# A two-layer transformer prompt on one core: PE transposes for the second unit's rows, held weight loads, new priorities

## The chip, the core and the metric

The program runs on one core of one Trainium2 chip. The time is device microseconds (us) of that core; the time of a kernel is the median over its runs. One further execution was recorded by the hardware profiler, and everything below that names an instant is an instant of that execution. Its engines are PE (TensorE matmul; its weight loads are shown apart as PEld), DVE (VectorE), ACT (ScalarE), POOL (GpSimd) and SP (SyncE, which here only issues transfers; ACT issues some as well).

## The reference

Two layers, each of them an attention block and a dense block on 2048 rows of 640 values:

```python
x = x + A(layernorm(x));  x = x + B(layernorm(x))      # twice, same weights

# A: 32 heads of 20, each row attends to itself and the 255 rows before it
qkv    = (x @ wqkv).reshape(B, S, 3, 32, 20)
scores = q @ k^T * 20 ** -0.5, masked to 0 <= i - j < 256
out    = (softmax(scores) @ v) @ wo

# B: squared ReLU
h   = relu(x @ w1 + b1) ** 2          # 640 -> 1536
out = h @ w2 + b2                     # 1536 -> 640
```

## The kernel before

**Units.** The work is cut into 16 units (`NU`): 2 layers times 8 groups of 256 rows (`T`). "The first unit" is unit 0. A unit goes through these stages. `layernorm` normalises its rows (two blocks of 128 rows). The rows are then transposed so that the 640 columns lie on the partitions, and split into a high and a low fp16 part (`yT`); each product below is three fp16 matmuls (`mm3`, L334). `stage_qk` computes q and k, which leave PSUM through one ACT and one DVE instruction (`high`, `low`, L534 and L537) into a staging tile, go to DRAM (`write`, L583 and L585) and come back in the layout of the heads (`spread`, L589). `stage_v` computes v. Attention runs in 8 "quads" of four heads: scores for the row maxima (`max_quad`, PE lines L703 and L735), the maxima sent into the q rows (`max_out` or `max_cross`, then `rows_out` L757), scores again and their exponentials (`exp_quad`: PE L840 and L886, ACT L825), masks on POOL or DVE, and the product with v (`pv_quad`, PE L931, then L943 and L946). The rows of the result go to DRAM (L951) and `load_o` brings them back (L984 the sums, L985 the rows) and divides by the sums in four slices (L1017, L1020, L1024, L1027: the job `od`). `stage_o` multiplies by `wo` and adds the residual (L1056); a second `layernorm`; a transposition into `y2` by `stage_y` or `y_cross`; `stage_f` is the dense block.

**Two ways to transpose.** `split_t` (L382) transposes on PE: five 128x128 transposes for a block of 128 rows, in tiles of three and two, into PSUM, and an ACT copy (L389) and a DVE subtraction (L390) take each tile out. `cross` (L443) writes the high part on ACT (L452) and the low part on DVE (L456) to a staging tile and transposes these with transfers issued by SP (L459). Before the change, unit 0 takes the first way (`ln_t(0)`), units 1 and 2 the second (`ln_early`).

**What sets the order.** All five engines run an order that is written out when the program is made. The program keeps a model of time: `post` adds a job with an engine, a cost, the jobs it depends on and a priority (`prio`; lower goes first); `pump` puts those jobs whose modelled start has come into the engine's stream. `dma` adds a transfer issued by SP, `bulk` a weight load issued by ACT, which is `idle`: it starts only when the modelled transfers are nearly done. The priorities are in the table `urgency` (L332), which is replaced once at unit 1 (L1381). The model decides only where an instruction stands in its engine's stream; what it waits for on the chip is its data and its tile.

**PSUM.** Results of the dense products and of `split_t` share two banks ("mm", `mm_tile` L240). PE can't begin a third until one of the two has been emptied.

**The dict `left`** (L540 to L555) holds, for a staging tile, the writes that must have left it before the next evictions overwrite it. Its test at L543 compares a pair with a tuple that holds a pair, which is never equal, so that in the model each piece of q (or k) of unit 0 waits for the write of the piece before it.

**Start and flow.** PE first runs `spin` matmuls without use. `load_wq` loads and converts the qkv weights (L285, L271, L272). `flow` (L1301) then runs the 8 quads of unit 0 (`todo`: maxima "m" three quads ahead, then "s" and "v") and, whenever the next step isn't ready in the model, takes a piece of the generator `rest` (`ahead_all`, L1350): q, k and v of units 0, 1 and 2 with the layernorms of units 1 and 2 between them. Under it, `load_wo`, `load_w1` and `load_w2` bring the other weights (ACT issues at L300, L309, L324). `load_w2` uses two places in the v tiles and three in the tile of unit 2's k rows; the latter is then filled with constants (`set_row`, L107) and with unit 2's k (L589). After `flow`, `load_o(0)` follows (L1368).

**From unit 1 on** (L1378), `together` runs the quads of unit u beside a chain of dense stages: for unit 1 `until(rest, ...)`, `stage_o(0)`, more of `rest`, `stage_y(0, ...)`, `stage_f(0)`; for units 2 to 14 `stage_qk` and `stage_v` of unit u+1 around `stage_o(u-1)` and `y_cross(u-1)`, then `stage_f(u-1)`. Unit 14 leaves `CARRY` ns of its dense work to unit 15; unit 15 spends it in portions: 10e3 (`MID`) before `stage_o(14)`, 4e3 after it, 2e3 between the two blocks of `stage_y(14)`, and what is left after the second block (L1392).

Of the kernel before, what the change touches and what calls it, by code (L numbers as in the profile page):

```python
# [16 lines left out]
P = 128  # L17
Q = P // 2
S = 2048
# [5 lines left out]
T = 256  # L25
# [6 lines left out]
NQ = H // 4  # L32
# [13 lines left out]
def kernel(ctx: ExitStack, tc: tile.TileContext, x, wqkv, wo, w1, b1, w2, b2, out):  # L46
# [70 lines left out]
    rate, apart, SWITCH = [335.0], [False], 110.0  # L117
    TAIL = {"A": 115.0, "D": 85.0, "G": 40.0, "S": 0.0}

    class Job:  # L120
        def __init__(self, eng, cost, fn, deps, nb, prio, size=0, idle=False, land=LAND):
            self.eng, self.cost, self.fn, self.deps, self.nb, self.prio = eng, cost, fn, deps, nb, prio
# [1 line left out]
            self.end, self.gates = None, []  # L124

        def ready(self):
            return all(d.end is not None for d in self.deps)

        def start(self):
            t = max([clk[self.eng], self.nb] + [d.end + LAT for d in self.deps])  # L130
            return max(t, moved[0] - 2200.0) if self.idle else t

        def put(self):
            t = self.start() + self.cost
# [194 lines left out]

    urgency = {"out": 0, "od": 1, "cross": 1, "mask": 0, "turn": 1, "exp": 1, "ln": 1, "y": 0.5, "clear": 0.5}  # L332

    def mm3(acc, lhs, rhs, nk, ns, then=None):  # L334

# [166 lines left out]
    def stage_qk(u, which=(0, 1)):  # L502
        js = pre.pop(u, ())
        yield Want(*js, bank=False)
        need(*js)
        yT = yTs[u]
        qds = {}

        order = [(j, c0) for j in which for c0 in range(0, KC, 2)]
        if u == 0:  # L510
            order.sort(key=lambda t: t[1])
        for j, c0 in order:
            if j not in qds:
                if j == 0:
                    qts[u] = sb.tile([P, NP, T], F16, name="qt", tag="qt", bufs=2)
                if j and u < 2:
                    qd, k = side(0), "side0"
                elif u == 2 and not j and opened0:
                    qd, k = side(1), "side1"
                elif j and u > 2:  # L520
                    qd = beside(u)[:, 1].rearrange("p (c a n) -> p c a n", a=2, n=T)
                    k = None
                else:
                    qd, k = sb.tile([P, KC, 2, T], F16, name="qd", tag="qd", bufs=1), "qd"
                qds[j] = qd, k
            qd, k = qds[j]
            dst = kts[u % 3] if j else qts[u]
            n = min(2, KC - c0)
            yield Want()
            acc, jobs = mm_tile([P, 2, T], "acc")  # L530
            s = QS / (YS * WS)

            def high(qd=qd, acc=acc, c0=c0, n=n):
                nc.scalar.activation(qd[:, c0:c0 + n, 0, :], acc[:, :n, :], AF.Copy, scale=s)  # L534

            def low(qd=qd, acc=acc, c0=c0, n=n):
                nc.vector.scalar_tensor_tensor(qd[:, c0:c0 + n, 1, :], acc[:, :n, :], s, qd[:, c0:c0 + n, 0, :],  # L537
                                               op0=ALU.mult, op1=ALU.subtract)

            def evict(wait, k=k, n=n, c0=c0, high=high, low=low, jobs=jobs, j=j, dst=dst, qd=qd):  # L540
                pr = urgency["out"]
                old = left.get(k, ())
                if k and (j, u) != old[:1]:  # L543
                    old = left[k] = ((j, u), [], old[1] if old else [])
                hi_ = post("A", 60 + 212 * n, high, *(old[2] if k else ()), wait=wait, prio=pr)
                lo_ = post("D", 70 + 267 * n, low, hi_, prio=pr)
                jobs.append(lo_)
                if u == 0:
                    wrote = leave(u, j, dst, qd, lo_, c0, n)
                elif c0 + n == KC:  # L550
                    wrote = leave(u, j, dst, qd, lo_, 0, KC)
                else:
                    return
                if k:
                    old[1].append(wrote)  # L555

            for c in range(n):
                lo = j * D + (c0 + c) * P
                need(wqj[lo // P])
                yield from mm3(acc[:, c, :], lambda a, k: wq_s[:, a, k, lo:lo + P],  # L560
                               lambda b, k: yT[:, b, k, :], KC, 109, evict if c == n - 1 else None)
# [11 lines left out]
    def leave(u, j, dst, qd, ready, c0, n):  # L573

        if c0 == 0:
            rows_of[u, j] = tc.dram_tile([D, 3, T], F16, name=f"qk{u}_{j}")
        dr = rows_of[u, j]
        drv = dr.rearrange("(c p) t n -> p c t n", p=P)

        p0, p1 = c0 * P // (2 * DH), (c0 + n) * P // (2 * DH)  # L580

        def write():
            nc.sync.dma_start(drv[:, c0:c0 + n, j:j + 2, :].rearrange("p c t n -> p c (t n)"),  # L583
                              qd[:, c0:c0 + n].rearrange("p c a n -> p c (a n)"))
            nc.sync.dma_start(drv[:, c0:c0 + n, 2 - 2 * j, :], qd[:, c0:c0 + n, 0, :])  # L585

        def spread():
            for e in range(2):
                nc.sync.dma_start(dst[64 * e:64 * e + 3 * DH, p0:p1, :],  # L589
                                  dr.rearrange("(p e d) t n -> e (d t) p n", e=2, d=DH)[e][:, p0:p1])  # L590

        wrote = dma(write, n * P * 3 * T * 2, ready, n=2, prio=0)

        def load(*deps):
            job = dma(spread, int((p1 - p0) * 2 * DH * 3 * T * 2 * (1.7 if u > 2 else 1.28)), wrote, *deps, n=2, prio=0)
            for p in range(p0, p1, 2):
                trips[u, j, p // 2] = job
            if u == 0 and j == 1 and p1 == NP:
                job.gates.append(gate)
            if u == 0 and j == 1 and p0 == 0:  # L600
                job.gates.append(gate0)

        if u == 2 and 2 not in rowset:
            held.append((j, load))
        else:
            load(*(rowset.get(u, ()) if j else ()))
        return wrote
# [361 lines left out]
    def load_o(u, late=False, free_=()):  # L969
# [15 lines left out]
            nc.sync.dma_start(val, ods[u][:DH].rearrange("(c d) h n -> (d h) c n", d=4))  # L985

        loaded = dma(load, P * (KC + 1) * T * 4, *wrote, *free_, n=2, prio=0)
        if u == NU - 1:
            both = sb.tile([P, 2, D], F32, name="x1", tag="qt", bufs=2)
            x1 = [both[:, i] for i in range(2)]  # L990
# [305 lines left out]
                if s.go() is None and not s.over:  # L1296
                    wait_any(s.want)

    QKC, VC, OC, FCST, LNC, CARRY, KEEP, MID = 16.4e3, 8.2e3, 8.2e3, 39.2e3, 1.2e3, 18e3, 24e3, 10e3

    def flow(todo, dense):  # L1301

# [2 lines left out]
        while todo:  # L1305
# [19 lines left out]
            elif kind == "s":  # L1325
                quad = exp_quad(n)
            else:
                pv_quad(n, quad)
            pump()

# [18 lines left out]

    def ahead_all():  # L1350
        yield from stage_qk(0)
        ln_early(1, place)
        yield from stage_v(0, range(2))
        ln_load(2)
        yield from stage_v(0, range(2, 4))
        ln_early(2)
# [14 lines left out]
    while not all(j.end is not None and j.end <= now[0] + LOOK for j in bbjobs):  # L1371
        c = next(rest)
        if not isinstance(c, Want):
            used[0] += c
            step(c)
    left_over = 3 * (QKC + VC) - used[0]
    rate[0] = 320.0
    for u in range(1, NU):  # L1378
        last = u == NU - 1
        if u == 1:  # L1380
            urgency.update({"out": 0, "od": 1.5, "cross": 1, "mask": 0, "turn": 0.7, "exp": 0.7, "ln": 0.5, "y": 1, "clear": 0.5})  # L1381
        quads, ahead = range(NQ * u, NQ * (u + 1)), range(NQ * u + LEAD, NQ * (u + 1) + LEAD)
        parts, cost, ahead_ln = [], OC + FCST, u + 2 if u + 2 < NU else None
        if 1 < u < NU - 1:
# [44 lines left out]
```

## Time and profile before

| | us |
|---|---|
| median of 3 runs | 1560.23 (1559.91 to 1561.74) |
| the profiled execution | 1561.46 |
| its span, first to last instruction | 1559.6 |
| so outside the span | 1.86 |

| engine | busy us | share |
|---|---|---|
| PE | 1533.5 | 98% |
| PEld | 1198.6 | 77% |
| DVE | 1043.3 | 67% |
| ACT | 669.7 | 43% |
| POOL | 451.8 | 29% |

A row of the timeline gives start, duration, engine, line, operation, output<-input and a count; the bracket at its end is the idle time of that engine before it and what ended it. A busy share says nothing about the clock: the windows view gives the granted TensorE clock (PEclk, 1.00 is full speed) of a stretch beside the busy time.

### The profile page before, as it was taken

How to read it: one execution, taken by the hardware profiler on the slowest of the kernel's cores; microseconds unless marked ns; L12 is line 12 of the kernel's file. 1: busy time of each engine (PE TensorE's matmuls, PEld its weight loads, DVE VectorE, ACT ScalarE, POOL GpSimd, SP SyncE). 2: the span in 40 equal slices, each digit the busy share in tenths (PEclk: the TensorE clock that was granted, in tenths of full speed). 3: DMA queues.
4: the chain of work that ended last, by engine and by line, in shares of the span. 5: the costliest groups of instructions: out<-in, count | busy, mean ns of one | idle time of the engine just before them, and what ended most of it. 6: DMA issues, size and time to landing. Idle time of an engine off the chain costs nothing. (4 is left out here: it accounts for less than half of the span.)

```text
span 1559.6 us, 58897 instructions
## 1 busy us (share of the span) xinstructions
PE 1533.5 (98%) x25822; PEld 1198.6 (77%) x25822; DVE 1043.3 (67%) x2244; ACT 669.7 (43%) x1365; POOL 451.8 (29%) x847
## 2 busy tenths in 40 slices
PE   8998999999999999999999999999999999999999
PEld 6666778787787877878777787877878777786777
DVE  8878775666757667675666757667675676667642
ACT  4565435334453443435343453444435335354422
POOL 1223314232141331413224141321413214142412
PEclk9999999999999999999999999999999999999999
DMA  9975354352534424344462434425243342542120
GB/s 271 209 201 127 80 121 92 106 114 54 123 88 114 105 74 126 69 126 89 99 130 63 119 91 119 100 70 132 67 126 89 94 117 65 122 90 59 30 68 18
DMA packets 248745, 162.16 MB, mean 104 GB/s; under 512 B 96552, under 2 KB 232232, under 8 KB 248488
## 3 DMA queue, kind: packets, MB, share of 16 engines
q1 hardware_dynamic: 242120, 148.89, 38.7%
q10 hardware_dynamic: 6368, 9.50, 2.1%
q8 instruction: 202, 3.31, 0.9%
q14 instruction: 55, 0.45, 0.1%
HBM read 84.68 MB, written 52.95 MB: 88 GB/s over the span
## 5 line engine op out<-in xcount | busy, mean ns | idle before, releaser
L825 ACT ACTIVATE pt<-bb 128x640 f32<-128x640 f32 (+2 forms) x512 | 311.9, 684 | 167.6 <-PE bb L840 148.9
L854 POOL TENSOR_SCALAR_AFFINE_SELECT pt<-pt 64x256 f32<-64x256 f32 x448 | 199.3, 445 | 582.1 <-ACT pt L825 560.0
L339 PE MATMUL acc<-y,w_s 128*128 128x256 f16 x2880 | 330.2, 274 | 1.2 <-DVE y L390 1.2
L339 PE MATMUL acc<-w_s,hh 128*128 128x320 f16 (+1 forms) x2340 | 326.7, 297 | 0.1
L339 PEld LDWEIGHTS <-w_s 128*128 128x128 f16 x2880 | 276.4, 98 | 40.9 <-issue 2.0
L339 PEld LDWEIGHTS <-hh 128*128 128x128 f16 x2340 | 222.1, 98 | 86.8 <-issue 0.4
L720 DVE TENSOR_REDUCE mx<-bb 128x4 f32<-128x1024 f32 x224 | 273.2, 1224 | 6.8
L339 PE MATMUL acc<-yT,wq_s 128*128 128x256 f16 x2250 | 259.1, 273 | 3.0 <-DVE qd L537 1.2
L339 PEld LDWEIGHTS <-wq_s 128*128 128x128 f16 x2400 | 229.6, 98 | 37.3 <-issue 4.3
L863 DVE COPY_PREDICATED_SCALAR pt<-drop,zero 128x256 f32 x224 | 99.9, 497 | 134.3 <-ACT pt L825 133.8
L1130 DVE TENSOR_TENSOR hh<-r,hh 128x256 f16<-128x256 f32 x192 | 98.3, 525 | 110.8 <-ACT hh L1127 105.7
L931 PE MATMUL pv<-pt,vt 64*32 64x192 f32 (+5 forms) x3840 | 166.7, 302 | 0.9 <-DVE y L390 0.6
L943 ACT COPY ot<-pv 128x256 f32<-128x256 f32 x128 | 47.6, 372 | 276.1 <-PE bb L931 247.2
L1124 POOL TENSOR_TENSOR r<-r 128x256 f32<-128x256 f32 x192 | 121.9, 655 | 127.9 <-ACT r L1120 125.3
L931 PE MATMUL bb<-pt,vt 64*32 64x128 f32 (+3 forms) x3584 | 153.5, 301 | 0.0
L717 DVE COPY_PREDICATED bb<-maskq,bb 128x256 f32<-128x256 uint16 x224 | 93.8, 423 | 85.7 <-PE bb L703 80.0
L931 PEld LDWEIGHTS pv<-pt,vt 64*32 64x32 f32 (+1 forms) x3840 | 125.5, 106 | 31.7 <-issue 3.7
L339 PE MATMUL acc<-wo_s,od 128*128 128x320 f16 x960 | 139.6, 299 | 2.2 <-ACT od L1024 2.0
L339 PE MATMUL acc<-wq_s,yT 128*128 128x320 f16 x900 | 132.1, 302 | 5.0 <-DVE qd L537 4.2
L1120 ACT ACTIVATE r<-acc,b1s 128x256 f32<-128x256 f32 x192 | 81.1, 476 | 98.6 <-PE acc L339 96.5
L339 PEld LDWEIGHTS <-od 128*128 128x128 f16 x960 | 90.9, 98 | 40.6 <-ACT od L1024 2.3
L339 PEld LDWEIGHTS <-yT 128*128 128x128 f16 x900 | 87.1, 98 | 40.0 <-issue 6.2
(103 smaller groups left out, 1476.3 us busy)
## 6 DMA issues: line engine op xcount, KB each, us to landing
qt<-qk SPq DMA_DIRECT2D x30, 480.0 KB
kt<-qk SPq DMA_DIRECT2D x30, 480.0 KB
o<-ot SPq DMA_DIRECT2D x256, 42.0 KB
qk<-qd SPq DMA_DIRECT2D x15, 640.0 KB
od<-o SPq DMA_DIRECT2D x14, 640.0 KB
qk<-yl SPq DMA_DIRECT2D x13, 640.0 KB
xt<-in_A_x_dram SPq DMA_DIRECT2D x16, 320.0 KB
x<-in_A_x_dram SPq DMA_DIRECT2D x16, 320.0 KB
```

The source lines that it names most:

```text
L339: nc.tensor.matmul(acc, lhs(a, c), rhs(b, c), start=(k == 0), stop=(k == 3 * nk - 1))
L717: nc.vector.copy_predicated(wins[:, :, 4 * Q:], later, wins[:, :, :Q])
L720: nc.vector.tensor_reduce(most, wins[:, :, Q:], axis=mybir.AxisListType.X, op=ALU.max)
L825: return lambda: nc.scalar.activation(room_of(box)[:, a:b], bank[:, a:b], AF.Exp, scale=SCALE / (QS * QS))
L854: nc.gpsimd.affine_select(out=m, in_=m, pattern=[[0, 4], [-1 if k else 1, Q]], base=0, fill=0.0, compare_op=ALU.is_gt if k else ALU.is_ge, ...
L863: nc.vector.copy_predicated(m, drop[:, k:k + 1, :].bitcast(mybir.dt.uint16).to_broadcast([P, 4, Q]), zero.unsqueeze(1).to_broadcast([P, 4, ...
L931: nc.tensor.matmul(pv[h][32 * jj:32 * (jj + 1), q0 * Q:(q0 + w) * Q], vf[r, c:c + 32], boxes[e]["pt"][r, a:b], start=(k == 0), stop=(k == ...
L943: nc.scalar.copy(ot[:, qd % 2], to)
L1120: nc.scalar.activation(box["r"], acc[:, f, :], AF.Relu, bias=b1s[:, f0 + f:f0 + f + 1], scale=1.0 / (YS * WS))
L1124: nc.gpsimd.tensor_tensor(box["r"], box["r"], box["r"], op=ALU.mult)
L1130: nc.vector.tensor_sub(hh[:, 1, f, :], box["r"], hh[:, 0, f, :])
```

## The change

The change has six parts.

1. The test at L543 now compares like with like: all pieces of one q (or k) share one entry, and wait only for the writes of the previous user of that staging tile.
2. In `ahead_all`, unit 1's rows are transposed by `ln_t(1, place)` on PE after the first half of `stage_v(0)`, in place of `ln_early(1, place)` (transfers) before it. Unit 2's still go by transfers. `left_over` grows by `LNC`.
3. A list `quiet` holds one empty job from the moment at which the last quad of unit 0 is about to be multiplied with v. `load_o(0)` ends it: the job's end is the modelled landing of the attention rows. Until then no `bulk` load is put into ACT's stream.
4. Writes of unit 2's q or k rows that are made while `quiet` has an entry wait for the same job.
5. Both tables of priorities change.
6. `CARRY` goes from 18e3 to 22e3.

```diff
+    quiet = []
...
         def ready(self):
-            return all(d.end is not None for d in self.deps)
+            return all(d.end is not None for d in self.deps) and not (self.idle and any(q.end is None for q in quiet))
...
-            return max(t, moved[0] - 2200.0) if self.idle else t
+            return max([t, moved[0] - 2200.0] + [q.end for q in quiet]) if self.idle else t
...
-    urgency = {"out": 0, "od": 1, "cross": 1, "mask": 0, "turn": 1, "exp": 1, "ln": 1, "y": 0.5, "clear": 0.5}
+    urgency = {"out": 0, "od": 0.5, "cross": 2, "mask": 0.5, "turn": 1, "exp": 1, "ln": 1, "y": 1, "clear": 0.5}
...
-                if k and (j, u) != old[:1]:
+                if k and (not old or old[0] != (j, u)):
                     old = left[k] = ((j, u), [], old[1] if old else [])
...
-        wrote = dma(write, n * P * 3 * T * 2, ready, n=2, prio=0)
+        wrote = dma(write, n * P * 3 * T * 2, ready, *(quiet if u == 2 else ()), n=2, prio=0)
...
         loaded = dma(load, P * (KC + 1) * T * 4, *wrote, *free_, n=2, prio=0)
+        if u == 0:
+            loaded.gates.append(quiet[0])
...
-    QKC, VC, OC, FCST, LNC, CARRY, KEEP, MID = 16.4e3, 8.2e3, 8.2e3, 39.2e3, 1.2e3, 18e3, 24e3, 10e3
+    QKC, VC, OC, FCST, LNC, CARRY, KEEP, MID = 16.4e3, 8.2e3, 8.2e3, 39.2e3, 1.2e3, 22e3, 24e3, 10e3
...
             else:
+                if n == NQ - 1:
+                    quiet.append(Job("S", 0.0, None, [], 0.0, 0))
                 pv_quad(n, quad)
...
         yield from stage_qk(0)
-        ln_early(1, place)
         yield from stage_v(0, range(2))
+        yield from ln_t(1, place)
         ln_load(2)
         yield from stage_v(0, range(2, 4))
         ln_early(2)
...
-    left_over = 3 * (QKC + VC) - used[0]
+    left_over = 3 * (QKC + VC) + LNC - used[0]
...
         if u == 1:
-            urgency.update({"out": 0, "od": 1.5, "cross": 1, "mask": 0, "turn": 0.7, "exp": 0.7, "ln": 0.5, "y": 1, "clear": 0.5})
+            urgency.update({"out": 0, "od": 1, "cross": 0.5, "mask": 0.5, "turn": 0.5, "exp": 0.7, "ln": 1, "y": 0.5, "clear": 0.5})
```

## The prediction

> **What bounds the kernel now.** I read the page first, its span and engines.
>
> ```profile
> span 1559.6 us, 58897 instructions
> PE 1533.5 (98%) x25822; PEld 1198.6 (77%) x25822; DVE 1043.3 (67%) x2244; ACT 669.7 (43%) x1365; POOL 451.8 (29%) x847
> ```
>
> PE is the bound and idles for 1559.6 - 1533.5 = 26.1 us. Only a change of PE's own work, of its idle time or of its clock can move the end; DVE and ACT matter where PE waits for them. The page's slices put the idle time at the start, so next came the windows of the first 320 us with their sum, and stretches of 2 us around the stalls (columns: length, busy time and count by engine, PEclk, DMA share, GB/s).
>
> ```profile
> sum 320.00, PE 304.83 PEld 234.29 DVE 242.37 ACT 150.02 POOL 85.42; mean PE 9.53 PEld 7.32 DVE 7.57 ACT 4.69 POOL 2.67
> 1420.00:1460.00 40.00, 36.17 (x738) 25.82 (x736) 31.85 (x65) 15.22 (x31) 8.29 (x18) 1.00 0.23 64
> 8.00:10.00 2.00, 1.89 (x17) 1.89 (x18) 1.04 (x3) 1.36 (x4) 0.00 (x0) 1.00 1.09 387
> 30.00:32.00 2.00, 0.00 (x0) 0.00 (x0) 1.26 (x4) 0.91 (x3) 0.41 (x1) 1.00 1.18 237
> 34.00:36.00 2.00, 2.00 (x14) 1.12 (x9) 1.77 (x13) 0.00 (x0) 0.00 (x0) 0.56 0.69 185
> 138.00:140.00 2.00, 0.45 (x32) 0.29 (x16) 1.97 (x3) 1.46 (x3) 0.55 (x1) 1.00 0.47 161
> 144.00:146.00 2.00, 2.00 (x11) 1.45 (x10) 1.97 (x5) 2.00 (x4) 1.11 (x1) 0.50 0.05 9
> ```
>
> 15.2 us of the idle time lie in the first 320 us and 3.8 in 1420 to 1460. Two places cost twice: PE stands still around 30 and 139, and some us later it is busy at a clock of 0.56 and 0.50. PE's timeline names them (the bracket is the idle time before the row).
>
> ```profile
> 7.27 1.61 PE L403 MATMUL bb<-ident,xt 128*128 128x128 f32 x10
> 33.06 0.70 PE L339 MATMUL acc<-wq_s,yT 128*128 128x320 f16 x4 [4.18 <-DVE qd L537]
> 34.13 4.43 PE L339 MATMUL acc<-wq_s,yT 128*128 128x320 f16 x19
> 38.93 2.75 PE L339 MATMUL acc<-wq_s,yT 128*128 128x320 f16 x19
> 129.86 0.75 PE L840 MATMUL bb<-qt,kt 62*64 62x128 f16 x37 [1.34 <-DVE ot L946]
> 137.09 0.37 PE L931 MATMUL pv<-pt,vt 64*32 64x256 f32 x1 [0.64 <-DVE y L390]
> 140.24 1.30 PE L403 MATMUL tr<-ident,xt 128*128 128x128 f32 x5 [1.78 <-DVE xt L378]
> 142.14 1.28 PE L840 MATMUL bb<-qt,kt 62*64 62x128 f16 x37 [0.36 <-DVE mx L720]
> 143.53 8.90 PE L339 MATMUL acc<-y,w_s 128*128 128x256 f16 x65
> 158.42 4.54 PE L339 MATMUL acc<-y,w_s 128*128 128x256 f16 x40
> 1457.80 0.77 PE L403 MATMUL tr<-ident,xt 128*128 128x128 f32 x5
> 1459.78 1.80 PE L339 MATMUL acc<-y,w_s 128*128 128x256 f16 x15 [1.21 <-DVE y L390]
> ```
>
> **Parts 1 and 2: the stall at 29 to 33.** The first v product needs one of the two "mm" banks, and these hold q's and k's last pieces. PE ended k's last piece at 33.06 - 4.18 = 28.9. Why the bank came free so late stands in ACT's and SP's timelines.
>
> ```profile
> 31.09 0.72 ACT L452 CAST stg<-xt 128x640 f16<-128x640 f32 x1 [2.76 <-DVE xt L378]
> 31.72 0.38 ACT L534 ACTIVATE qd<-acc 128x256 f16<-128x256 f32 x1
> 28.35 4.69 SPq L459 DMA_TRANSPOSE kt<-stg  x3
> ```
>
> The evictions L534 stand in ACT's stream behind L452, the cast of unit 1's second block, which waits for that block's layernorm. ACT was idle for 2.76 us with the evictions due. Both reasons for this order go: the model no longer holds a piece for the write of the piece before, and L452 of unit 1 doesn't exist. The first bank is then emptied beside k's last matmuls. I take off the whole 4.18. Nineteen matmuls took 4.43 at the low clock, 2.75 at the full one, so the drop cost another 1.7: together **-5.9**. If evictions still come late, by DVE's conversions for example, the gain is between 0 and 5.9.
>
> SP loses four transposing transfers (4.69 for three, so 1.56 each with waits); the reads of unit 0's q and k rows stand behind these. That starts attention sooner, but it saves no PE time while PE is full: 0. DVE and ACT lose two L452 and two L456 and gain four L389 and four L390 of about half the size: 0.
>
> Added on PE are ten transposes (five for each of two blocks), by the row at 1457.80 at 0.77 for five: **+1.6**, inside a stream that PE has to run. `flow` passes over a generator's wish to wait, so PE stands while a tile is emptied by L389 and L390. The trace has this for other units: 0.64 at 137.09 and 1.21 at 1459.78. Two such waits lie between 0 (scores happen to fall there) and 2.4; I take 0.64 twice, since there too attention stands between the tiles: **+1.3**. Unit 1's layernorm itself can't be what is late: its last step ended before the cast at 31.09, and PE gets there after 30 v matmuls, at 28.9 + 30 x 0.145 (2.75 / 19) = 33.3.
>
> The Trainium skill, page "TensorE: Matmul & The Clock Gate", section "Part 4: PE-mode transpose", says that transposes don't count as PE activity for the clock, which would speak against more of them. No run here shows that alone: ten transposes ran from 7.27 to 8.88, and the clock is 1.00 in the slice 8 to 10. I leave it out of the sum and name its case below.
>
> **Parts 3 and 4: 104 to 147.** These are SP's and ACT's issues, the first use of the attention rows on DVE and on PE, and the sizes of two transfers from the page.
>
> ```profile
> 104.21 1.01 ACTq L324 DMA_DIRECT2D kt<-in_B_w_dram  x2
> 104.60 2.64 SPq L951 DMA_DIRECT2D o<-ot  x4
> 110.26 0.59 SPq L984 DMA_DIRECT2D rs<-o  x1
> 110.94 0.43 SPq L985 DMA_DIRECT2D od<-o  x1
> 111.47 0.47 SPq L583 DMA_DIRECT2D qk<-qd  x1
> od<-o SPq DMA_DIRECT2D x14, 640.0 KB
> qk<-qd SPq DMA_DIRECT2D x15, 640.0 KB
> 116.00:118.00 2.00, 2.00 (x29) 1.33 (x29) 1.97 (x4) 0.44 (x1) 0.00 (x0) 1.00 1.10 357
> 117.03 0.54 DVE L1017 RECIPROCAL rs<-rs 128x64 f32<-128x64 f32 x1
> 122.54 1.80 PE L339 MATMUL acc<-wo_s,od 128*128 128x320 f16 x12
> ```
>
> Unit 0's last rows are written at 104.60 beside two weight loads, and their landing takes until 110.26; their reading (640 KB) then shares full DMA engines (1.10) with the writes of unit 2's rows: 640 KB by L583 and, by the code, half as much by L585. At 357 GB/s 640 KB alone last 1.8 us, with 960 KB beside them 4.5. So holding those makes the rows an estimated 2.5 us earlier, and holding the two loads something under the 3 us between the end of SP's issue (107.2) and 110.26; I take 3.5 in all, between 0 and 5.5. In the model `od` also has a better priority.
>
> What does PE gain? Nothing at once: `until` fills this wait with `rest`, and before the change `rest` was used up when `stage_o(0)` began. After it PE has nothing to put before `stage_y(0)`'s layernorms and waits 1.34, 0.64, 1.78 and 0.36 us, and then runs slowly: five transposes 1.30 for 0.77 (0.5), scores 1.28 for 0.75 (0.5), 65 matmuls 8.90 for 65 x 4.54 / 40 = 7.4 (1.5), so 2.5. If `od` is ready 3.5 us sooner, 3.5 us of `rest` remain, and the two `until` behind `stage_o(0)` spend it just there. I take off the 1.78, the 2.5 of clock, and half of the 1.34 (L946, with priority "turn", goes ahead of the layernorm from unit 1 on): **-5.0**. The tile waits 0.64 and 0.36 stay. Bounds: 0 to 6.6.
>
> What the hold delays: weight loads behind it on ACT. The two at 104.21 would come an estimated 10 us later.
>
> ```profile
> 125.43 0.82 DVE L272 SCALAR_TENSOR_TENSOR w_s<-kt,w_s 128x640 f16<-128x640 f32 x1
> 161.68 0.91 SPq L589 DMA_DIRECT2D kt<-qk  x2
> 172.97 0.76 PE L703 MATMUL bb<-kt,qt 60*64 60x256 f16 x38
> ```
>
> Their conversion came only at 125.43, so this has cover. Behind the last conversions unit 2's k rows are read at 161.68, needed for scores at 172.97; if weights become later by more than 10 us, that cover is gone, and PE first takes dense work: 0 to +5, I take 0. Unit 2's q rows are due at 172.97 too: 0.
>
> **Part 6.** Unit 15's portions are 10 + 4 + 2 = 16 us; with 18 little was left behind `stage_y(14)`, and PE waited 1.21 at 1459.78. With 22 about 4 us more remain there: **-1.2** (0 to -1.2). Unit 14's quads then have 4 us less beside them; I count nothing.
>
> **Part 5, units 2 to 13.** PE has next to no idle time there, so no priority can win much (of the 26.1 us, 26.1 - 15.2 - 3.8 = 7.1 are left for all of it and the very end). Layernorm goes behind the maxima on DVE, its cross goes ahead of other work: 0, with the loss in the third rival.
>
> **Sum.** -5.9 + 1.6 + 1.3 - 5.0 - 1.2 = -9.2. From the profiled execution's 1561.46 (span 1559.6 and 1.86 around it) that is 1552.3. The median stands 1.23 below that execution, so I forecast **1551.0**.
>
> **Rivals.**
> 1. The second stall stays (0.20). What PE lacked at 140 was the second block's layernorm behind other DVE work, not `od`; DVE was busy for 1.97 of 2 us there. The first stall's gain alone: 1551.0 + 5.0 = 1556.0.
> 2. The first stall stays since the v product waits for something else, say conversions (0.07): 1551.0 + 5.9 = 1556.9. That is also the case in which part 1 doesn't do what it says.
> 3. Slower (0.10): the transposition of y becomes late in every unit from 2 to 14, since L369, L370 and L378 go behind L720.
>
> ```profile
> 235.03 1.23 SPq L459 DMA_TRANSPOSE y<-yl  x1
> 242.41 4.00 PE L339 MATMUL acc<-y,w_s 128*128 128x256 f16 x35
> L720 DVE TENSOR_REDUCE mx<-bb 128x4 f32<-128x1024 f32 x224 | 273.2, 1224 | 6.8
> ```
>
> The last transfer's issue ends at 236.3, its use is at 242.4; with some 1.4 us to land, an estimate, 4.7 are spare. Each L720 that passes it costs 1.22, so it decides from the fourth on; five are 6.1 - 4.7 = 1.4 us in 13 units, 18.2: 1569.2. Against it: the cross's own jobs move up.
> 4. The clock drops behind the new transposes (0.08): 1.7 to 2.5 as above, 1553.1 here.
> 5. Weights and k rows late, at +5 (0.05): 1556.0.
>
> **Numbers.** My forecast has 0.50, with a range of its own of 1548 to 1554. The whole range takes in the kept stalls with the dearer tile waits (1556.9 + 1.1, and 1.2 without part 6, so about 1560) and, below, the 26.1 us' smaller stalls: **1545.5 to 1560.0**; the slower rival is left out. 0.2% is about what a measurement of this kernel can tell from no change: 1557.1 to 1563.4. Faster 0.76 (forecast, rival 4, most of 1, half of 2 and 5), same 0.13, slower 0.11.
>
> **What would show it.** No wait over 1 us of L339 for L537 near 30 and a clock of 1.00 at 34 to 38 (parts 1 and 2); ten L403 between v matmuls with two waits for L390; L985 followed by L1017 within 4 us and qkv matmuls between the two blocks of `stage_y(0)`, clock 1.00 at 135 to 145 (parts 3 and 4); dense work after unit 14's last transposes (part 6). I am wrong if `rest` runs out again before `stage_y(0)`, if ACT's evictions stand behind something else, or if new waits of L339 for y or yT repeat in the units from 2 on.

## The result and the profile after

The changed kernel is slower: 1571.27 us median (1566.27 to 1573.17, 6 runs) against 1560.99 (1559.05 to 1564.36, 6 runs) on the same chip, a ratio of 1.0061 with a 95% interval of 1.0043 to 1.0079. The profiled execution took 1569.6 us with a span of 1567.8. The two profiled executions differ by 1567.8 - 1559.6 = 8.2 us in span; the ratio makes the difference 9.5 (6.7 to 12.3). The six times of the changed kernel lie 6.9 us apart, so where lengths taken from one execution each differ by 1 or 2 us below, that alone shows nothing. Lines of the changed kernel stand 2 to 4 higher than before (L339 is L341, L840 is L842, L946 is L948).

The page of the changed kernel:

```profile
span 1567.8 us, 58967 instructions
PE 1537.6 (98%) x25832; PEld 1203.2 (77%) x25832; DVE 1047.7 (67%) x2246; ACT 669.7 (43%) x1367; POOL 452.5 (29%) x847
```

PE has ten matmuls more, the transposes. Its idle time went up, from 26.1 to 1567.8 - 1537.6 = 30.2 us. To see where, I cut each span in three: up to unit 1's dense block, from there to unit 12's, and the rest. The marks are the first matmul of a dense block, so PE has done the same work up to each of them, but for the ten transposes. First the windows of the kernel before, then of the changed one (columns: length, busy time and count by engine, PEclk, DMA share, GB/s).

```profile
0.00:242.41 242.41, 227.56 (x3405) 173.69 (x3405) 190.17 (x466) 118.36 (x232) 61.80 (x123) 0.98 0.66 167
242.41:1283.85 1041.44, 1038.45 (x17992) 815.17 (x17991) 692.63 (x1459) 440.70 (x902) 305.39 (x572) 1.00 0.41 99
1283.85:1559.61 275.76, 267.50 (x4434) 209.79 (x4428) 160.48 (x321) 110.68 (x231) 84.59 (x152) 1.00 0.26 65
```

```profile
0.00:242.77 242.77, 226.84 (x3415) 174.13 (x3415) 189.81 (x468) 117.96 (x234) 59.69 (x123) 0.98 0.62 164
242.77:1292.48 1049.71, 1041.93 (x17995) 817.79 (x17990) 698.62 (x1459) 441.85 (x902) 308.12 (x572) 1.00 0.41 99
1292.48:1567.79 275.31, 268.87 (x4434) 211.30 (x4428) 159.25 (x321) 109.92 (x231) 84.69 (x152) 0.99 0.26 66
```

The first stretch was to lose 8 us and came out 0.36 longer. The middle, which I had priced at nothing, grew by 8.27: 4.79 of PE's idle time (7.78 for 2.99) and 3.48 of its busy time. The end is 0.45 shorter. So there are two questions: who ate the gain in the first stretch, and what is late in the middle.

**The first stretch.** Windows again, at the first stall and from 104 to the end of the stretch, cut at unit 0's dense block (143.53 before, 142.82 after); before and after:

```profile
28.00:60.00 32.00, 26.97 (x245) 18.41 (x243) 23.46 (x98) 10.65 (x23) 5.88 (x11) 0.95 0.99 213
104.00:143.53 39.53, 34.69 (x636) 25.16 (x632) 35.82 (x71) 20.90 (x41) 7.35 (x14) 0.96 0.63 164
143.53:242.41 98.88, 98.88 (x1819) 77.60 (x1817) 72.75 (x141) 44.72 (x88) 32.36 (x56) 0.98 0.43 98
```

```profile
28.00:60.00 32.00, 29.67 (x286) 21.92 (x284) 27.62 (x111) 15.04 (x32) 5.45 (x11) 1.00 1.05 253
104.00:142.82 38.82, 31.52 (x559) 21.84 (x554) 31.82 (x62) 18.50 (x36) 8.36 (x15) 0.87 0.64 167
142.82:242.77 99.95, 98.58 (x1857) 77.30 (x1856) 72.11 (x141) 43.78 (x88) 29.06 (x55) 1.00 0.38 90
```

In 28 to 60 the idle time fell from 5.03 to 2.33 us and the low clock went (0.05 x 32 = 1.6 us lost before, none after): a gain of 4.3. Behind 104 both got worse. Idle time went from 4.84 (and none behind 143.53) to 7.30 + 1.37 = 8.67, which is 3.8 more. The clock has to be followed past that mark, since before the change its drop behind the second stall runs on into unit 0's dense block: 0.04 x 39.53 + 0.02 x 98.88 = 3.6 us lost before, 0.13 x 38.82 = 5.0 after. So a gain of 4.3 at the first stall stands against a loss of 5.2 behind 104. By the clock's record in the traces, half speed lasts 3.41 us behind the first stall and 6.83 behind the second before the change, and 6.83 from 118.5 and 3.41 from 139.0 after it: 10.24 us in both kernels. The balance doesn't close: with the 1.6 of the transposes the stretch should be 2.5 us longer, and it is 0.36. One reason is that some of the low clock now falls on time in which PE stands and loses nothing by it; the rest is not followed.

PE's timeline of the changed kernel at the first stall:

```profile
33.39 0.44 PE L405 MATMUL tr<-ident,xt 128*128 128x128 f32 x2 [0.20 <-ACT vt L624]
34.56 0.77 PE L405 MATMUL tr<-ident,xt 128*128 128x128 f32 x5 [0.73 <-DVE kt L392]
36.26 2.74 PE L341 MATMUL acc<-wq_s,yT 128*128 128x320 f16 x19 [0.49 <-DVE kt L392]
```

The wait of 4.18 for `qd` is gone. The first row of transposes, three from 32.70, has no wait; the waits that the transposes bring are 0.20 + 0.73 + 0.49 = 1.42. The nineteen matmuls behind them take 2.74, which is full speed. Now the second stall, first the matmuls of `rest` before the change, then the changed kernel:

```profile
104.05 4.54 PE L339 MATMUL acc<-yT,wq_s 128*128 128x256 f16 x40
109.21 2.75 PE L339 MATMUL acc<-wq_s,yT 128*128 128x320 f16 x19
114.52 3.30 PE L339 MATMUL acc<-wq_s,yT 128*128 128x320 f16 x23
118.55 0.57 PE L339 MATMUL acc<-wq_s,yT 128*128 128x320 f16 x3
119.39 2.20 PE L339 MATMUL acc<-wq_s,yT 128*128 128x320 f16 x15 [0.28 <-DVE mT L795]
```

```profile
104.30 4.25 PE L341 MATMUL acc<-wq_s,yT 128*128 128x320 f16 x30
109.17 3.30 PE L341 MATMUL acc<-wq_s,yT 128*128 128x320 f16 x23
114.46 0.58 PE L341 MATMUL acc<-wq_s,yT 128*128 128x320 f16 x3
116.87 0.76 PE L842 MATMUL bb<-qt,kt 62*64 62x128 f16 x37 [1.67 <-DVE ot L948]
119.76 0.37 PE L705 MATMUL bb<-kt,qt 60*64 60x256 f16 x1 [1.93 <-ACT pt L827]
121.57 8.12 PE L341 MATMUL acc<-wo_s,od 128*128 128x320 f16 x45
137.06 0.27 PE L705 MATMUL bb<-kt,qt 60*64 60x256 f16 x1 [2.42 <-ACT pt L827]
```

Before the change 4.54 + 2.75 + 3.30 + 0.57 + 2.20 = 13.4 us of `rest` were left at 104 for the gaps between the attention steps; in the changed kernel 4.25 + 3.30 + 0.58 = 8.1. What PE saved at 30 it spent at once on `rest`, while unit 0's attention reached 104 no sooner. The dense work ran out at 115, and PE stood 1.67 and 1.93 us for attention where it had had matmuls to run. `stage_o(0)` begins at 121.57 for 122.54, one microsecond earlier, and its 45 matmuls take 8.12 us: the clock had fallen, as the windows show (0.50 from 120 to 124). PE stands once more, 2.42 us up to 137.06, and the clock falls again (0.50 from 140 to 142). A window at the first of these drops:

```profile
120.00:122.00 2.00, 1.77 (x40) 1.24 (x39) 1.40 (x4) 1.00 (x3) 1.80 (x4) 0.50 0.79 143
```

Why the attention rows help so little, though parts 3 and 4 were to clear the queue ahead of them, stands in SP's and DVE's timelines of the changed kernel:

```profile
104.70 0.40 SPq L585 DMA_DIRECT2D qk<-qd  x1
105.82 3.16 SPq L953 DMA_DIRECT2D o<-ot  x4
111.42 0.49 SPq L987 DMA_DIRECT2D od<-o  x1
116.41 0.41 DVE L948 TENSOR_TENSOR ot<-bb,ot 128x256 f32<-128x256 f32 x1
116.74 0.81 DVE L274 SCALAR_TENSOR_TENSOR w_s<-kt,w_s 128x640 f16<-128x640 f32 x1
118.39 0.94 DVE L1021 RECIPROCAL rs<-rs 128x64 f32<-128x64 f32 x2
```

The load is issued at 111.42, where it was issued at 110.94 before, since unit 0's last rows were written no sooner: SP issues their writes (L953) at 105.82, before the change at 104.60. Ahead of them now stand the last writes of unit 2's rows (L585 at 104.70, L587 at 105.14), which followed the load at 111.47 before. `rest` is further on here, and part 4 had nothing left to hold. By the counts of its semaphore the load had landed by 116.63, and by 116.88 before. DVE takes the rows up at 118.39, behind unit 1's maxima, L948, a conversion of weights (L274) and two steps that send the maxima on (L796, L797); before it did so at 117.03.

**The middle.** PE's waits in the middle stretch, before and after (total, times, longest):

```profile
PE bb L840 <- issue: 2.3, 3, 1.1
PE bb L840 <- DVE ot L946: 0.3, 1, 0.3
```

```profile
PE bb L842 <- DVE ot L948: 4.3, 5, 1.1
PE bb L842 <- issue: 1.8, 1, 1.8
PE bb L933 <- DVE mx L685: 0.9, 1, 0.9
```

Scores wait for L948, the sum of the two halves of the product with v, five times. In the wait followed here L948 is not slow itself: it stands in DVE's stream behind maxima, and these behind something that comes late. The second of the five, followed back, in rows of DVE, SP, POOL, DVE and PE; first before the change:

```profile
421.78 0.60 DVE L378 TENSOR_SCALAR xt<-x,bmv 128x640 f32<-128x640 f32 x1
433.54 0.44 SPq L1069 DMA_DIRECT2D xt<-in_B_b_dram  x1
438.67 0.86 POOL L1076 TENSOR_TENSOR x<-x,xt 128x320 f32<-128x320 f32 x1 [8.16 <-DMA xt<-in_B_b_dram]
444.89 1.43 DVE L1130 TENSOR_TENSOR hh<-r,hh 128x256 f16<-128x256 f32 x2 [1.44 <-ACT hh L1127]
449.87 0.79 PE L840 MATMUL bb<-qt,kt 62*64 62x128 f16 x38
```

```profile
424.50 1.23 DVE L722 TENSOR_REDUCE mx<-bb 128x4 f32<-128x1024 f32 x1
426.26 0.61 DVE L380 TENSOR_SCALAR xt<-x,bmv 128x640 f32<-128x640 f32 x1
427.82 3.43 SPq L461 DMA_TRANSPOSE y<-yl  x2
435.84 0.44 SPq L1073 DMA_DIRECT2D xt<-in_B_b_dram  x1
440.56 0.86 POOL L1080 TENSOR_TENSOR x<-x,xt 128x320 f32<-128x320 f32 x1 [9.43 <-issue]
446.63 1.42 DVE L1134 TENSOR_TENSOR hh<-r,hh 128x256 f16<-128x256 f32 x2 [1.92 <-ACT hh L1131]
451.63 0.76 PE L842 MATMUL bb<-qt,kt 62*64 62x128 f16 x37 [0.86 <-DVE ot L948]
```

The changed kernel is 0.7 us behind at this unit. The layernorm's last step (L380) now waits behind maxima (L722) and comes 4.5 us later; the transposing transfers behind it hold SP's queue until 431; the load of the bias b2 goes out 2.3 later, and the adding of b2 on POOL, which stands ahead of the squares of the dense block, 1.9 later. Squares, their low parts (L1134), the maxima behind those and L948 follow, and PE's scores wait 0.86. y itself was there in time. The other four waits are not followed row by row. But against the first matmul of its unit's dense block, the load of b2 goes out later than before in ten of the eleven units of this stretch, by 0.2 to 1.8 us.

### The profile page after: what moved, and what is told of

The parts are those of the page before. It is cut to its first block, busy times and chain, and to the rows that moved or that the text cites. A ratio compares the mean times of both kernels' runs of the same rounds, so it can differ in the third digit from the quotient of the medians.

```text
span 1567.8 us, 58967 instructions
## 1 busy us (share of the span) xinstructions
PE 1537.6 (98%) x25832; PEld 1203.2 (77%) x25832; DVE 1047.7 (67%) x2246; ACT 669.7 (43%) x1367; POOL 452.5 (29%) x847
## 4 chain that ended last, share of the span: by engine, by line
PE 87%; DVE 4%; issue 3%; ACT 2%; DMA 2%; POOL 2%; SPq 1%; ACTq 0%; DVEq 0%; POOLq 0%
PE acc L341 67%; PE pv L933 7%; PE bb L842 5%; PE bb L705 5%; PE bb L933 2%; ACT pt L827 1%; DVE mx L722 1%; DVE bb L685 1%; POOL pt L856 1%; POOL r L1128 1%; DMA kt<-qk 0%; DVE bb L719 0%; PE bb L737 0%; PE bb L888 0%; DMA xt<-in_B_b_dram 0%
## 5 line engine op out<-in xcount | busy, mean ns | idle before, releaser
L341 PE MATMUL acc<-y,w_s 128*128 128x256 f16 x2880 | 329.5, 273 | 3.4 <-DVE y L392 1.7
L341 PE MATMUL acc<-w_s,hh 128*128 128x320 f16 (+1 forms) x2340 | 326.9, 297 | 0.0
L341 PEld LDWEIGHTS <-w_s 128*128 128x128 f16 x2880 | 276.0, 98 | 43.1 <-issue 4.6
L341 PEld LDWEIGHTS <-hh 128*128 128x128 f16 x2340 | 221.8, 98 | 86.8 <-issue 0.8
L722 DVE TENSOR_REDUCE mx<-bb 128x4 f32<-128x1024 f32 x224 | 274.0, 1223 | 7.1
L341 PE MATMUL acc<-yT,wq_s 128*128 128x256 f16 x2250 | 259.0, 273 | 1.1 <-DVE wq_s L274 0.6
L341 PEld LDWEIGHTS <-wq_s 128*128 128x128 f16 x2400 | 229.6, 98 | 35.6 <-issue 2.6
L1134 DVE TENSOR_TENSOR hh<-r,hh 128x256 f16<-128x256 f32 x192 | 101.1, 536 | 122.3 <-ACT hh L1131 116.5
L933 PE MATMUL pv<-pt,vt 64*32 64x192 f32 (+5 forms) x3840 | 171.1, 304 | 0.0
L933 PE MATMUL bb<-pt,vt 64*32 64x192 f32 (+3 forms) x3584 | 157.3, 302 | 0.9 <-DVE mx L685 0.9
L933 PEld LDWEIGHTS pv<-pt,vt 64*32 64x32 f32 (+1 forms) x3840 | 128.8, 106 | 28.8 <-issue 2.9
L341 PE MATMUL acc<-wo_s,od 128*128 128x320 f16 x960 | 140.2, 302 | 0.0
L341 PE MATMUL acc<-wq_s,yT 128*128 128x320 f16 x900 | 130.2, 299 | 1.0 <-DVE kt L392 0.5
L341 PEld LDWEIGHTS <-od 128*128 128x128 f16 x960 | 92.0, 99 | 38.3 <-issue 0.4
L933 PEld LDWEIGHTS bb<-pt,vt 64*32 64x32 f32 x3584 | 117.6, 106 | 3.8 <-issue 1.3
```

What stands on the lines that cost most here:

```text
L341: nc.tensor.matmul(acc, lhs(a, c), rhs(b, c), start=(k == 0), stop=(k == 3 * nk - 1))
L722: nc.vector.tensor_reduce(most, wins[:, :, Q:], axis=mybir.AxisListType.X, op=ALU.max)
L933: nc.tensor.matmul(pv[h][32 * jj:32 * (jj + 1), q0 * Q:(q0 + w) * Q], vf[r, c:c + 32], boxes[e]["pt"][r, a:b], start=(k == 0), stop=(k == ...
L1134: nc.vector.tensor_sub(hh[:, 1, f, :], box["r"], hh[:, 0, f, :])
```

## The experiments

Three lengths in brackets stand for the three stretches of that kernel's profiled execution; before they are [242.4, 1041.4, 275.8], after [242.8, 1049.7, 275.3]. Ratios are to the kernel before, with 95% intervals. Only one execution is behind each set of lengths.

**The second table alone**, put into the kernel before:

```diff
-            urgency.update({"out": 0, "od": 1.5, "cross": 1, "mask": 0, "turn": 0.7, "exp": 0.7, "ln": 0.5, "y": 1, "clear": 0.5})
+            urgency.update({"out": 0, "od": 1, "cross": 0.5, "mask": 0.5, "turn": 0.5, "exp": 0.7, "ln": 1, "y": 0.5, "clear": 0.5})
```

> The kernel before with the second table of priorities alone (from unit 1 on). Theory A, the second table costs the time: between the first dense blocks of units 0 and 14 the time grows by about 7 us (1316.3 before, 1323.7 after), with several waits of the scores' PE line for the sum of the two halves of pv (7 such waits, 7.2 us, in the changed kernel), and the whole is about 1568. Theory B, the parts before unit 1 shift everything behind them and the table does nothing: 1559 to 1562. My prediction's sum had 0 for it: 1560.2.

1582.49 us, ratio 1.0133 (1.0117 to 1.0149), [243.4, 1056.1, 282.7]. PE's waits of L840 for L946 are 5.2 us in seven times. That is far more than the 1568 of theory A: the middle grows by 14.6 and the end by 7. The middle's loss is the table's.

**The changed kernel with both tables as they were** (`CARRY` stays at 22e3):

> The changed kernel with both old tables of priorities. Theory A: the 7 us behind unit 0 go away, about 1563; if the second stall is then as in the changed kernel nothing is won at the start. Theory B: as the changed kernel, about 1571.

1574.54 us, 1.0084 (1.0070 to 1.0098), [246.3, 1043.1, 285.5]. Neither theory has this time. The middle is nearly back at 1041.4, and the end has grown by 10. With the old table and 22e3, PE is left without work at unit 15's second layernorm, as a row of its timeline near the end shows; with 18e3 the end is 276.0 (`e14_no_tables` below).

```profile
1529.08 0.77 PE L405 MATMUL bb<-ident,xt 128*128 128x128 f32 x5 [3.35 <-DVE xt L380]
```

**Part 1 alone**, put into the kernel before:

```diff
-                if k and (j, u) != old[:1]:
+                if k and (not old or old[0] != (j, u)):
```

> The kernel before with the corrected test on the staging tiles alone (part 1). My prediction: the wait of 4.18 us at 33 goes with its 1.7 us of low clock, 1554 to 1555. Theory C, unit 0's attention and not PE sets when its first 150 us end, so that rest is merely used up sooner: the wait goes, but new idle time of about the same size appears between 104 and 145, and the time is within 2 us of before.

1576.78 us, 1.0099 (1.0085 to 1.0113), [257.1, 1041.8, 276.5]. Both accounts missed: 1554 to 1555, and within 2 us of before. The wait at 33 is gone with part 1 alone, though unit 1's casts (L452) are still there: the eviction L534 now stands ahead of them, at 28.17. In its place PE waits 2.86 us for `qd` at 49.53, and the clock falls behind that. The first stretch is 14.7 us longer, with 8.0 more of idle time, spread over many places. One of them is the fifth rival's: unit 2's k rows are asked for at 176.46 instead of 161.68, and PE waits for them.

```profile
185.01 0.65 PE L703 MATMUL bb<-kt,qt 60*64 60x128 f16 x33 [2.46 <-DMA kt<-qk]
```

In the changed kernel nothing of this is left. The parts don't add up one by one.

**Parts 1 and 2 together**, put into the kernel before (the diff's lines at L543, in `ahead_all`, and `left_over`):

> The kernel before with parts 1 and 2 (corrected test, and unit 1's rows transposed on PE). My prediction: -5.9 and +2.9, about 1557. Theory C: the last quad of unit 0 meets v within 1 us of where it did (103.0), and less than 13 us of q, k and v matmuls are left behind it, so PE idles more between 104 and 145: 1559 to 1563.

1564.61 us, 1.0019 (1.0011 to 1.0028), [244.9, 1041.2, 275.1]. The first stall is gone here too, and the first stretch is 2.5 us longer, not 3 shorter. So the loss of the first gain needs neither the hold nor the new priorities.

**The second table's entries**, in groups, each put into the kernel before: `turn` 0.5 with `ln` 1; then `cross` 0.5 with `y` 0.5 and `od` 1; then `mask` 0.5; and `ln` 1 alone:

```diff
-"turn": 0.7, ... "ln": 0.5
+"turn": 0.5, ... "ln": 1
```

> The kernel before with two entries of the second table: turn 0.5 (was 0.7) and ln 1 (was 0.5), the order on DVE. The whole second table made the stretch from the first dense block of unit 1 to that of unit 12 14.6 us longer (1041.4 to 1056.1) and the stretch from there to the end 7 us longer. If the order on DVE between maxima and layernorm is the cause (my third rival's mechanism), nearly all of the 14.6 shows here; if POOL's or the transposing transfers' order is, less than 3.

```diff
-"od": 1.5, "cross": 1, ... "y": 1
+"od": 1, "cross": 0.5, ... "y": 0.5
```

> The kernel before with cross 0.5, y 0.5 (were 1) and od 1 (was 1.5) in the second table: casts and subtractions for the transposing transfers, and the division of the attention rows, go ahead of the dense block's own work on ACT and DVE. If these are the cause, nearly all of the 14.6 us between units 1 and 12 shows here; else less than 3.

```diff
-"mask": 0
+"mask": 0.5
```

> The kernel before with mask 0.5 (was 0) in the second table: on POOL the masks go behind the squares of the dense block. In the changed kernel POOL adds b2 before the masks and squares later, ACT's and DVE's casts of the dense block come 1 us later, and with them the maxima, the sum of pv and PE. If that order is the cause, most of the 14.6 us between units 1 and 12 shows here; else less than 3.

```diff
-"ln": 0.5
+"ln": 1
```

> The kernel before with one entry of the second table, ln 1 (was 0.5): the layernorm's steps go behind the maxima on DVE, as in my third rival. e5_dve (ln and turn) made the stretch from unit 1's to unit 12's first dense block 11.0 us longer. If ln is what does it, about 1052 for that stretch; if turn is, within 1.5 of 1041.4.

The first: 1572.41 us, 1.0069 (1.0054 to 1.0084), [243.3, 1052.4, 276.3]. The second: 1566.43, 1.0035 (1.0025 to 1.0044), [241.4, 1047.1, 276.2]. The third: 1562.28, 1.0005 (0.9996 to 1.0015), [241.8, 1041.6, 275.2]: nothing. The last: 1573.43, 1.0073 (1.0054 to 1.0092), [243.7, 1060.3, 276.9]; the profiled execution was the slowest of its runs, so its middle is an upper end. `ln` alone is enough for the loss of its group. The second group, without `ln` and `turn`, costs 5.7 in the middle by itself; how it does so was not followed. The run with `ln` also shows SP's part of the chain of above by itself (kernel before with `ln` at 1):

```profile
428.62 3.29 SPq L459 DMA_TRANSPOSE y<-yl  x2
436.54 0.44 SPq L1069 DMA_DIRECT2D xt<-in_B_b_dram  x1
```

**More or less of PE's work in the first stretch.** To see whether PE's work or attention sets the pace there: 24 useless matmuls of 128x128 in `rest`, behind unit 1's transposes, in the kernel with parts 1 and 2; and the changed kernel with unit 2's v from the high parts alone, which leaves out 40 of its 60 matmuls (and some of the value's accuracy).

```diff
+    def spare_work(pieces, n):
...
         yield from ln_t(1, place)
+        yield from spare_work(4, 6)
...
```

> Parts 1 and 2 (as e4_fix_pe, 1564.6), with 24 matmuls of 128x128 without use added on PE behind the new transposes, 5.2 us of PE by the row of the first spin matmuls (6.01 us for 28). Theory C, unit 0's attention sets when the first 145 us end and PE only uses rest up sooner or later: within 2 us of 1564.6, the idle time at 110 to 130 shrinks by about as much. If PE is what bounds there, 1569.7.

```diff
...
-            for a, b in ((0, 0), (0, 1), (1, 0)):
+            for a, b in pairs:
...
+                               ((0, 0),) if u == 2 else ((0, 0), (0, 1), (1, 0)))
...
```

> The changed kernel with v of unit 2 from its high parts alone (20 matmuls of 60; the low parts of rows and weights are left out there), so that PE has 40 x 0.146 = 5.8 us less work, the last of rest, around 103 to 115. Theory C, the start of unit 0's dense block (142.8 us) is set by a chain of latencies (unit 0's quads until 103.5, its rows through DRAM, the division on DVE, stage_o, two layernorms): it stays within 1.5 us of 142.8, and PE idles 4 to 6 us more before it; the whole is within 2.5 us of the changed kernel's 1571.3. If PE's work sets it, it comes at 137.0 and the whole at 1565.5.

The first took 1587.26 us, 1.0164 (1.0147 to 1.0180), but is no clean test: the order shifted so that unit 1's k rows, asked for at 85.63, were waited for until 96.94. The second took 1572.90, 1.0075 (1.0059 to 1.0092), [250.2, 1048.5, 274.0]. With less work `stage_o(0)` begins at 121.29 for 121.57: up to there PE's work doesn't set the pace, and it waits instead. The first dense block comes later (145.17 for 142.82, where the expectation allowed 1.5), since PE waits for the residual's sums:

```profile
PE acc L341 <- DVE x L1061: 4.8, 1, 4.8
```

That wait is not attention's: DVE's L1061 at 131.37 had stood 3.46 us for the residual's own rows (`x<-in_A_x_dram`), asked for at 121.87 for 120.95. So what less work for PE would bring at the dense block stays open.

**`CARRY` back at 18e3 in the changed kernel:**

```diff
-    ... LNC, CARRY, ... = ... 1.2e3, 22e3, ...
+    ... LNC, CARRY, ... = ... 1.2e3, 18e3, ...
```

> The changed kernel with CARRY back at 18e3. With the old tables 22e3 made the stretch from the first dense block of unit 12 to the end 10 us longer (275.2 in e4_fix_pe, 285.5 in e2_after_old_tables); with the new tables and 18e3 it is 282.8 (e1_table1), with both new 275.3. So if the two only fit together, this run loses about 7 us: that stretch about 283, the whole 1578. My prediction's sum had part 6 alone at -1.2, so +1.2 here: 1572.5.

1574.68 us, 1.0088 (1.0073 to 1.0103), [242.9, 1051.0, 280.5], with 283 expected for the end. So 22e3 helps the end by 5 with the new table and harms it by 10 with the old one. The middle stays long (1051.0), so its loss doesn't come from `CARRY`.

**`turn` and `ln` of the second table back in the changed kernel:**

```diff
-"turn": 0.5, ... "ln": 1
+"turn": 0.7, ... "ln": 0.5
```

> The changed kernel with turn 0.7 and ln 0.5 back in the second table, the rest as changed. If the order on DVE costs the time in the middle, the stretch between units 1 and 12 falls from 1049.7 to at most 1047.1 (e6_cross) and the waits of the scores for the sum of pv go away there; but the stretch after unit 12 may grow as in e2_after_old_tables, by up to 10.

1581.37 us, 1.0133 (1.0118 to 1.0148), [245.7, 1047.0, 287.0]. PE's waits for L948 in the middle fall from 4.3 us in five times to 0.9 in one, but the middle falls only by 2.7, to the level of the other group (1047.1). The end is 11.7 longer, as it was by 10 with both old tables and this `CARRY`.

**The changed kernel without the second table**, `CARRY` at 18e3 (`mask` stays at 0.5, which had moved nothing); the same without either table; and the first of these with the division taken up earlier, by letting the model count half the bytes:

```diff
-        loaded = dma(load, P * (KC + 1) * T * 4, *wrote, *free_, n=2, prio=0)
+        loaded = dma(load, P * (KC + 1) * T * (2 if u == 0 else 4), *wrote, *free_, n=2, prio=0)
```

> The changed kernel with CARRY at 18e3 and the second table as it was, but for mask at 0.5, which alone moved nothing. Theory A (what the changed kernel loses is the second table's crossing and layernorm priorities, in units 2 to 13): the stretch from unit 1's dense block to unit 12's is 1041.5 +- 1 us (1049.7 in the changed kernel, 1041.5 before), the rest is within 1.5 us of the changed kernel's, and the time is 1560 to 1562, the same as before. Theory B (the parts can't be told apart: any new order loses some 8 us somewhere): the stretch is 1046 or more, or another one grows by as much, and the time stays above 1566.

> The changed kernel with both tables and CARRY as before, so that parts 1 to 4 are left: the held loads and writes on top of the kernel with parts 1 and 2, which took 1564.6. My first account (the hold brings the attention rows 3.5 us earlier to DVE and saves 5 us): 1559 to 1560. The account from the traces (the rows land earlier, DVE takes them up no earlier, and no dense work is saved): the first dense block begins at 144.5 to 146, the time is 1563 to 1566, and the end stretch is at 275, not 285, since that came from CARRY at 22e3 with the old table.

> As e13_no_table2, but the model counts half the bytes for the load of unit 0's attention rows, so that its division stands earlier in DVE's stream. If the late start of the division on DVE is what keeps the second stall, the first reciprocal comes before 117, stage_o(0) begins 1.5 to 3 us earlier than in e13, dense work is left before the first dense block, and that block begins 2 us or more earlier: 1557 to 1559 in all, faster than before. If unit 0's attention sets the pace whatever the division does, the block begins within 0.7 us of e13's: 1560 to 1562. If the rows come too late for it, DVE stands and the maxima are delayed: slower than e13 by 1 to 3.

The first: 1564.88 us (1563.91 to 1566.35), 1.0025 (1.0016 to 1.0034), [245.6, 1042.4, 276.0]. The middle's windows and PE's waits there:

```profile
245.61:1288.01 1042.40, 1039.79 (x17996) 815.95 (x17991) 695.26 (x1459) 440.78 (x902) 306.76 (x572) 1.00 0.41 99
PE bb L842 <- issue: 2.2, 3, 0.9
```

No wait for L948 is left, and the stretch is within 1 us of before: the middle's loss in the changed kernel is the second table's. The time itself missed its expectation by 3; the first stretch is 2.8 longer than in the changed kernel. The same difference stands between the kernels with the table whole (242.8 and 242.9) and those with at least its `turn` and `ln` undone (245.6, 245.7, 246.3): here the table seems to gain some 3 us in unit 1 (five executions, one of each kernel) and loses 7 in units 2 to 12. The second: 1565.27, 1.0025 (1.0015 to 1.0035), [247.1, 1041.9, 276.0]. Against parts 1 and 2 alone (1.0019) the hold of parts 3 and 4 brings nothing, where 1559 to 1560 was expected if it did. The third: 1564.25, 1.0021 (1.0012 to 1.0031), [245.4, 1043.5, 276.6]. It is no test of what it was meant for: the first reciprocal stands at 119.07, as without the edit (119.06), and `stage_o(0)` at 122.25 for 122.24. Unit 0's dense block begins at 142.67 for 145.82, but unit 1's at 245.4 for 245.6. Whether an earlier division would win anything stays open.

## Why the prediction was wrong, step by step

- **The first stall (-5.9) and its price (+1.6 and +1.3): right.** The wait for `qd` and the low clock behind it are gone, the waits for tiles are 1.42 for 1.3, and 28 to 60 gained 4.3 for 5.9 - 1.3 = 4.6. Of the two reasons given, part 1 alone is enough (`e3_fix`). The clock stayed at 1.00 over the ten transposes, so the fourth rival fell.
- **"If `od` is ready 3.5 us sooner, 3.5 us of `rest` remain" (-5.0): failed, and took the first gain with it.** Two things were wrong. The rows came no 3.5 us sooner: the load was issued 0.5 later, landed 0.25 earlier and was taken up by DVE 1.4 later, and `stage_o(0)` began 1.0 earlier. The writes of unit 2's rows, whose hold was to bring 2.5 of the 3.5, had gone out ahead of unit 0's last rows. And the sum took the amount of `rest` at 104 as fixed. It isn't: `flow` puts `rest` wherever PE would stand, so what is saved at 30 is `rest` that is missing at 115 (8.1 us left at 104 for 13.4), unless attention comes sooner too. It didn't. I had answered "Nothing at once" to what PE gains from earlier rows; the same answer held for the first stall, and I didn't apply it there. Measured, in place of 5.0 us less: 3.8 us more of idle time and 1.4 more of low clock behind 104. That the dense work ran out is what the traces show; that the first dense block would come sooner with faster attention was not shown (`e15_od_soon` didn't speed it up). The sign named for being wrong, `rest` running out again before `stage_y(0)`, came. The first rival had the second stall stay too, but kept the first stall's gain.
- **Part 5, "no priority can win much ... 0": failed.** The bound on the gain was right (7.1 us of idle time). The loss was the third rival's, which I gave 0.10 and 1569.2. Its cause holds in part (layernorm behind the maxima on DVE: `ln` alone costs as much as its group), its place doesn't: I looked for late transposes of y. These had enough time in the wait that was followed. (The time to spare was less than I had counted: the transfer of the row at 235.03 landed 3.1 us behind the end of its issue, by its semaphore, and not 1.4.) What was late is what SP, in order, issues behind them, the load of b2, and then POOL, DVE and the scores. Measured: 8.3 in the middle in the changed kernel, and 14.6 in the kernel before. That the table is the cause is shown (`e1_table1`, `e13_no_table2`); how much of it `turn` and `ln` carry depends on the rest: 11.0 of 14.6 in the kernel before, but only 2.7 come back with `turn` and `ln` undone in the changed one, and the path from `cross`, `y` and `od` to PE stays open. Of the 8.3, 4.8 are idle time of PE. The other 3.5 are longer busy time for the same work: 2.6 in the products with v (116.46 to 119.06 us), 0.4 in the scores' line L842, 0.25 each in L341 and L888. A product near 761 takes 1.96 us for 1.37; why others do, stays open.
- **Part 6 (-1.2): right in sign, and only beside the new table.** The end is 0.45 shorter, less than one execution can show; against 18e3 in the changed kernel it is 5 shorter. With the new table and 18e3 the end is 5 longer than before (`e10_carry18`; 7 in `e1_table1`), with the old one and 22e3 10 (`e2_after_old_tables`). That the two fit together was no part of the working.
- **Weights and k rows late (+5):** not in the changed kernel, but in the one with part 1 alone.

Together: -8.0 expected in the first stretch and +0.4 measured, 0 expected in the middle and +8.3 measured, -1.2 and -0.45 at the end. No version of these beats the kernel before.

## What to carry to other kernels

Where a filler stream (work put wherever the engine would stand) covers the waits of a chain, removing one wait of the filler's engine moves that wait to the place where the filler runs out, unless the chain itself ends sooner: count what filler is left at the last place that needs it. A priority that lets one job slip is to be followed down every in-order queue behind that job, to the last job that shares it, and not only to the job's own user. Parts of a change that was tuned as a whole, such as a table and an amount carried over, are to be tried together and apart, since their effects here had different signs alone.

## What the hardware showed

The granted clock falls to half for 3.41 us or for twice that: 3.41 behind the first stall and 6.83 behind the second before the change, 6.83 from 118.5 and 3.41 from 139.0 after it. A drop of 3.41 us in which PE is busy so costs 1.7. The Trainium skill, page "TensorE: Matmul & The Clock Gate", section "Part 1: The HAM clock gate (the "warmup" mystery)", has a free-running window of about 3.4 us and half speed after an idle one; half of 3.4 is 1.7, and the sizes agree. But the window before the drop at 118 wasn't idle: between waits of 1.67 and 1.93 us PE ran 38 matmuls of scores and a transpose, and the clock still fell. In the 3.41 us up to each of the four drops PE was busy for 1.19 and 1.36 us before the change (30.83 to 34.25, 136.65 to 140.06), and for 1.07 and 1.60 after it (115.10 to 118.51, 135.58 to 138.99). Short matmuls between waits of under 2 us didn't keep the clock up; how much would have was not measured.
